# Half 0's tile table begun right behind its row numbers, its VectorE operations at low rank in the plan

## The chip, the cores and the metric

The kernel runs on one core of one Trainium2 chip. The metric is the device time of one execution in microseconds (us). The engines are named as in the profile: PE is TensorE's matmuls and PEld its weight loads, DVE is VectorE, ACT is ScalarE, POOL is GpSimd, SP is SyncE, which here only issues DMAs and reads registers. SBUF is the on-chip working memory, PSUM the small memory that PE writes its products to.

## What is computed

Attention, then a mixture of eight experts with one expert for each token, then a dense layer pair:

```python
x = attn(rotate(q), rotate(k), v)            # B, H, S, D = 2, 8, 576, 64
x = x.transpose(0, 2, 1, 3).reshape(1152, 512)
logits = x @ w_gate + modality_bias[modality_id]
e_idx = argmax(logits, axis=1)               # one of 8 experts
for e in range(8):                           # h: 512 x 1024, then 1024 x 512
    mask = e_idx == e
    out[mask] = gate_w[mask] * (relu(x[mask] @ w1[e]) @ w2[e])
h = out @ w_in                               # 512 x 2048
return (h * tanh(softplus(h))) @ w_out       # 2048 x 512
```

All in float32; products run as sums of a rounded high part and a low part ("hi" and "lo").

## The kernel before

**Stages.** Sixteen heads of attention (heads 0 to 7 are half 0 of the tokens, heads 8 to 15 half 1), then the experts for half 0 and half 1 (two tiles of 304 rows each, L712), then the dense pair (L1588, L1649).

**One head.** POOL prepares its inputs: `p_mul` (L924, 128x1152), `p_add` (L928), `p_hi` and `v_hi` (L934), `p_lo` (L943), `v_lo` (L968), all from SBUF to SBUF; `p_lo` of head n is the plan's operation ("plo", n). Then PE forms the scores (`sc`, L979) in one of two PSUM tiles, DVE takes each row's maximum (`nm`, L1003), ACT the exponential (`pexp`, L1014). PE transposes it into a buffer of a ring of three in PSUM (`pt`, L1027), ACT writes the rounded part (`ph`, L1047), DVE the rest (`pl`, or the lower rows of `ph`, L1053), which gives the ring's buffer back, and PE multiplies with the values (`av`, L1068). The same ring holds the small product `xo` (L1098), which DVE reads at L1108. POOL adds to the sums of the exponentials (`rs`, L1086).

**The plan.** The order of the attention's instructions on every engine is made ahead of the run by `Plan`, a list scheduler with assumed durations, due times (`K`) and dependencies; engines run what they are given strictly in that order. Besides its operations the plan has streams: generators that yield one step at a time. A stream whose engine is in `low` gets a slot there only if its step is thought to be over, with 0.1 us to spare, before the next operation could start:

```python
if c is None or t + (st["next"][1] - P["slack"] if e in st["low"] else 0.0) <= c[0]:
    c = (t, 0, st)
```

**Routing of half 0.** When heads 0 to 7 are done, `routing(0)` finds each token's expert and its row in a sorted buffer `scratch` (up to L404, "row numbers"); POOL then scatters the rows to it by five indirect DMAs (L410), and DVE makes the tile table `tbl` (L433 to L523), eighteen small operations on one partition: which expert and which rows each tile has. SP reads the table into registers (L555, L556) and loads rows and weights (`weights()`), when the table, the scatters and the last head's loads are done.

Up to the row numbers the intermediate tiles lie in PSUM where `near` puts them; behind `side = False` (L428) `near` returns a tile of pool `rp`, so that all tiles of half 0's table (`ce`, `n1`, `qi`, `stq`, `lt`, `te`, `cs`) and its constants (`zero`, `iotat`, `iota8`, `base`) are in SBUF:

```python
def near(sh, nm):
    if not side:
        return t(sh, nm)
    ...
    v = cur["rtile"][0:sh[0], o:o + n]
```

For half 1 (`side` stays true) most of them are views of a PSUM tile. Two tensors of SBUF are read by L439 (`ce`, `n1`), L447 (`n1`, `zero`), L453 (`qi`, `n0`), L455 (`st`, `base`), L481 (`qi`, `iotat`), L492 (`iota8`, `e8`), L497 (`lt`, `st`) and L502 (`iotat`, `cs`) of half 0; the ten others read one.

Of the kernel before, what the change touches and what calls it, by code (L numbers as in the profile page):

```python
# [18 lines left out]
B, H, S, D = 2, 8, 576, 64  # L19
# [193 lines left out]
def moe_kernel(ctx: ExitStack, tc: tile.TileContext, aps, out):  # L213
# [17 lines left out]
    def heads(x):  # L231

        return x[..., 0:XC].rearrange("p j (h e) -> p j h e", h=H)
# [343 lines left out]
    def load_rows(k):  # L577
        r = regs[k]
        pool = mp if k != "x" else wpool[-1]
        xrow[k] = t = pool.tile([128, 3, RW], F32, tag="xrow", name=f"xrow{k}")  # L580
        for i, (r0, rn) in enumerate(TCH):
            ld = nc.sync.dma_start(out=t[:rn, i], in_=scratch[ds(r["c"] + r0, rn), :])
            if k != "x":
                after_scatters(ld, k[0])
# [240 lines left out]


    def attention(actx, hook):
        a_c = actx.enter_context(tc.tile_pool(name="a_const", bufs=1))
        p2 = actx.enter_context(tc.tile_pool(name="a_p2", bufs=2))
# [404 lines left out]
        op("ids", "act", 0.1, 30.0, setup_ids)  # L1234
        op("bias", "pool", 2.5, 60.0, setup_bias, deps=[("ids",)])
        hook(plan, bank, ltile)
        plan.run()

# [12 lines left out]
    def route(b):  # L1251
        yield from routing(b, lambda: cur["rbank"]())

    def tile_rows(b):
        for i in range(2):
            regs[b, i] = tile_regs(tbl[b][:, i])

    def until_pe(gen):
        for y in gen:
            if y[0] in ("pe", "mark"):  # L1260
                return
            yield y

    def hook(plan, bank, ltile):

        r0 = route(0)
        cur["rbank"] = lambda: bank("counts")

        def until_mark():
            for y in r0:  # L1270
                if y[0] == "mark":
                    return
                yield y

        def mark(name):
            return lambda t: plan.done.update({name: ("dve", t)})

        def start():
            plan.add(until_pe(r0), plan.now, end=mark("rt"), gate=cur["spare"])

        def rest():
            next(r0)
            plan.add(until_mark(), plan.now + 1.0, end=mark("rt_row"))

        def scatter():
            plan.add(cur["scatters"], plan.now, low=("pool",), end=mark("rt_sc"))

        def table():
            plan.add(r0, plan.now, end=mark("rt_end"))

        def weights():
            tile_rows(0)
            load_rows(K0)
            feed.rows.add(K0)
            plan.done["xrow"] = ("sp", plan.now + 7.8)
            plan.add(until_pe(gen0), plan.now + 3.9, low=LOW)

        K0, n0, xg = (0, 0), B * H - 1, []

        def x_gate(i):  # L1300
            x, rn = xrow[K0], TCH[i][1]
            if not xg:
                gated.add(K0)
                t = mp.tile([128, FC1, T], F32R, tag="hl", name=f"xg{K0}").bitcast(F32)
                xg.append(t.rearrange("p a t -> p (a t)")[:, 0:3 * DM].rearrange(
                    "p (i d) -> p i d", i=3
                ))
            nc.vector.tensor_scalar(
                out=xg[0][:rn, i].rearrange("p (h e) -> p h e", h=H),
                in0=heads(x)[:rn, i, :, 0:D], scalar1=x[:rn, i, XC + 1:XC + 2], scalar2=None,  # L1310
                op0=ALU.mult,
            )

        def x_bank(c):
            return ltile[3 + c // 2][:, c % 2]

        def x_tr(c, i):
            r0, rn = TCH[i]
            nc.tensor.transpose(
                out=x_bank(c)[:, r0:r0 + rn], in_=xg[0][:rn, i, c * 128:(c + 1) * 128],  # L1320
                identity=ident[:rn, :rn],
            )

        def x_hi(c):
            if K0 not in xsplit:
                xsplit[K0] = tuple(
                    mp.tile([128, KC, T], F32R, tag=t, name=f"{t}{K0}") for t in ("xh", "xl")
                )
            nc.scalar.activation(out=xsplit[K0][0][:, c], in_=x_bank(c)[:, :T], func=AF.Copy)

        def x_lo(c):
            xh, xl = xsplit[K0]
            nc.vector.tensor_tensor(
                out=xl[:, c], in0=x_bank(c)[:, :T], in1=xh[:, c].bitcast(F32), op=ALU.subtract
            )

        def x_op(name, eng, dur, fn, *a, deps):
            plan.op((name,) + a, eng, dur, 900.0, lambda: fn(*a), deps=deps)

        for i in range(3):  # L1340
            plan.op(
                ("gate", i), "dve", 0.5, (162.0, 165.0, 150.0)[i], lambda i=i: x_gate(i),
                deps=["xrow"],
            )
        for c in range(KC):
            for i in range(3):
                x_op("xtr", "pe", 0.11, x_tr, c, i,
                     deps=[("gate", i), ("exp", n0, 1, c // 2, 3 + c // 2)])
            x_op("xhi", "act", 0.31, x_hi, c, deps=[("xtr", c, i) for i in range(3)])
            x_op("xlo", "dve", 0.39, x_lo, c, deps=[("xhi", c)])  # L1350

        z = 10.0 * H
        plan.op(
            "route", "sp", 0.0, z, start,
            deps=[("norm", n, f) for n in range(H) for f in range(2)],
        )
        plan.op("rt_mm", "pe", 0.43, z, lambda: next(r0), deps=["rt"], take=[("ring", "rt")])
        plan.op("rt_cp", "dve", 1.1, z, rest, deps=["rt_mm"], give=[("ring", "rt")])
        plan.op("scatter", "sp", 0.0, z, scatter, deps=["rt_row"])
        plan.op("table", "sp", 0.0, z, table, deps=["rt_row", ("plo", B * H - 1)])  # L1360
        plan.op(
            "rows", "sp", 2.2, z, weights,
            deps=["rt_end", "rt_sc", ("stack", B * H - 1), ("vload", B * H - 1)],
        )
# [14 lines left out]
    with ExitStack() as actx:  # L1379
        attention(actx, hook)  # L1380
# [414 lines left out]
```

## Time and profile before

| what | value |
|---|---|
| median of 3 runs | 485.11 us (484.85 to 485.18) |
| the profiled execution's own time | 485.32 us |
| its span, first to last instruction | 483.6 us |
| PE, DVE, ACT, POOL busy, us of the span | 464.2, 390.4, 331.2, 361.9 |
| half 0's row numbers ready (L397 on DVE) | 110.72 us |
| half 0's table, first and last operation | 134.29 and 145.52 us |
| last product of the attention on PE begins | 162.71 us |
| first matmul of the experts (L712) begins | 163.17 us |

Times of rows are counted from the start of the span. A row of the timeline gives start, duration, engine, line, operation, output<-input and count of merged instructions; what stands in brackets is idle time of the engine ahead of it and what ended it. Rows of one engine can overlap, since it starts the next instruction before the last one's writes have landed.

### The profile page before, as it was taken

To read this page: it belongs to the slowest core of one execution; us is meant where nothing else is said; L and a number is where in the kernel's file an instruction comes from. 1 tells how busy PE (TensorE), PEld (TensorE's weight loads), DVE (VectorE), ACT (ScalarE), POOL (GpSimd) and SP (SyncE) were. 2 spreads that over 40 slices of the span, in tenths; PEclk is the share of its full clock that TensorE was granted. 3 is DMA by queue.
4 is the path that set the end of the run, shared out by engine and by line. 5 is a ranking of instruction groups with operands and counts; after the bars stand their busy time and mean duration, and the time that the engine had idled before them with its cause. 6 is when DMAs were issued, how large, how long until landed. Compare 5 with 4: busy or idle time off the path is not lost.

```text
span 483.6 us, 8783 instructions
## 1 busy us (share of the span) xinstructions
PE 464.2 (96%) x2996; PEld 427.7 (88%) x2996; DVE 390.4 (81%) x616; ACT 331.2 (68%) x753; POOL 361.9 (75%) x363
## 2 busy tenths in 40 slices
PE   2799999999999999999999999999999999999995
PEld 1699999999998999999999998989889887888894
DVE  6599899798898765655888689999999859777773
ACT  3588888777878665475554587666675788776763
POOL 3799999999981588768767277786786749987654
PEclk9999999999999999999999999999999999999999
DMA  7689985877765399977974400202000001100002
GB/s 225 168 200 243 224 239 149 193 205 178 182 162 171 136 386 385 330 300 262 378 279 186 174 2 1 79 10 87 1 0 1 1 1 43 45 22 1 1 0 89
DMA packets 24131, 69.41 MB, mean 144 GB/s; under 512 B 5522, under 2 KB 9810, under 8 KB 22034
## 3 DMA queue, kind: packets, MB, share of 16 engines
q1 hardware_dynamic: 21794, 63.16, 42.1%
q0 software_dynamic: 1456, 5.03, 2.7%
q10 hardware_dynamic: 832, 0.61, 0.5%
q8 instruction: 25, 0.41, 0.3%
q14 instruction: 24, 0.20, 0.1%
HBM read 49.08 MB, written 6.44 MB: 115 GB/s over the span
## 4 chain that ended last, share of the span: by engine, by line
PE 41%; DVE 8%; issue 3%; POOL 1%; ACT 1%; POOLq 0%; DVEq 0%; ACTq 0%
PE h L1588 15%; PE o L1649 15%; PE mm L712 11%; DVE ta L1614 6%; DVE wc L1418 1%; DVE ta L1615 1%; POOL out_dram L1659 0%; DVE wc L1408 0%; PE mm L675 0%; DVE wc L1413 0%; POOLq L1791 0%; POOL g L1632 0%; DVE idi L1735 0%; ACT ot L1655 0%; DVE yl L1526 0%
## 5 line engine op out<-in xcount | busy, mean ns | idle before, releaser
L1614 DVE RECIPROCAL ta<-ta 128x320 f32<-128x320 f32 (+1 forms) x64 | 124.6, 1947 | 21.5 <-ACT ta L1607 20.0
L1562 POOL TENSOR_TENSOR w2l<-wc,w2h 128x512 fp32r<-128x512 f32 x64 | 89.3, 1417 | 15.3 <-ACT w2h L1561 15.3
L1649 PE MATMUL o<-w2h,g 128*128 128x512 f32 x288 | 97.8, 395 | 0.1
L1632 POOL TENSOR_TENSOR g<-ta,g 128x320 fp32r<-128x320 f32 (+1 forms) x63 | 52.7, 841 | 27.9 <-ACT g L1626 21.3
L979 PE MATMUL sc<-sk,sq 128*128 128x288 f32 (+1 forms) x320 | 59.4, 315 | 11.5 <-ACT sk L908 7.7
L1588 PE MATMUL h<-yl,w2h 128*128 128x320 f32 (+2 forms) x204 | 67.0, 328 | 0.1
L1588 PE MATMUL h<-yh,w2h 128*128 128x320 f32 (+2 forms) x204 | 66.9, 328 | 0.0
L1588 PE MATMUL h<-yh,w2l 128*128 128x320 f32 (+2 forms) x204 | 66.9, 328 | 0.0
L1649 PEld LDWEIGHTS o<-w2h,g 128*128 128x128 f32 x288 | 53.9, 188 | 12.2 <-POOL g L1632 1.0
L1047 ACT ACTIVATE ph<-pt 128x512 fp32r<-128x512 f32 (+2 forms) x112 | 54.8, 509 | 13.4 <-PE pt L1027 12.4
L1014 ACT ACTIVATE pexp<-sc,nm 128x576 f32<-128x576 f32 x72 | 53.3, 740 | 15.5 <-DVE nm L1003 11.7
L1003 DVE TENSOR_REDUCE nm<-sc 128x1 f32<-128x576 f32 x72 | 53.7, 753 | 10.8 <-PE sc L979 6.7
L979 PEld LDWEIGHTS sc<-sk,sq 128*128 128x128 f32 (+1 forms) x320 | 46.6, 190 | 14.3 <-ACT sk L908 8.1
L1649 PE MATMUL o<-w2l,g 128*128 128x512 f32 x144 | 56.8, 394 | 0.0
L1027 PE MATMUL pt<-ident,pexp 128*128 128x128 f32 (+1 forms) x360 | 55.0, 277 | 0.7 <-DVE tbl L523 0.6
L1068 PE MATMUL av<-ph,vhl 128*128 128x256 f32 (+1 forms) x160 | 50.7, 333 | 0.0
L1053 DVE TENSOR_TENSOR pl<-pt,ph 128x512 fp32r<-128x512 f32 (+1 forms) x80 | 48.8, 628 | 2.1 <-ACT ph L1047 1.8
L1027 PEld LDWEIGHTS pt<-ident,pexp 128*128 128x128 f32 (+1 forms) x360 | 42.1, 138 | 3.6 <-issue 0.7
L1626 ACT ACTIVATE g<-ta 128x320 fp32r<-128x320 f32 (+1 forms) x64 | 27.9, 436 | 22.9 <-DVE ta L1615 22.5
L1603 ACT ACTIVATE ta<-h 128x320 f32<-128x320 f32 (+1 forms) x64 | 25.5, 399 | 25.0 <-PE h L1588 23.5
L1588 PEld LDWEIGHTS h<-yl,w2h 128*128 128x128 f32 x204 | 38.3, 188 | 4.1 <-DVE yl L1526 0.4
L1588 PEld LDWEIGHTS h<-yh,w2h 128*128 128x128 f32 x204 | 38.3, 188 | 3.9 <-DVE ta L1615 0.2
(448 smaller groups left out, 1203.7 us busy)
## 6 DMA issues: line engine op xcount, KB each, us to landing
wr<-in_wio_dram SPq DMA_DIRECT2D x16, 1024.0 KB, 6.1
wc<-in_w_dram SPq DMA_DIRECT2D x26, 512.0 KB, 5.7
xs<-in_qk_dram SPq DMA_DIRECT2D x15, 576.0 KB, 5.2
sk<-ab SPq DMA_DIRECT2D x30, 288.0 KB, 3.3
sq<-ab SPq DMA_DIRECT2D x30, 144.0 KB, 2.4
vraw<-in_v_dram SPq DMA_DIRECT2D x16, 160.0 KB, 3.9
scratch<-zero SPq DMA_DIRECT2D x12, 108.8 KB, 4.8
xrow(0, 0)_2295<-scratch SPq DMA_DIRECT2D x2, 290.0 KB, 3.1
```

The costliest lines, as they stand in the source:

```text
L712: nc.tensor.matmul(ps[:, :T], lhsT=w, rhs=m, start=(n == 0), stop=(n == 3 * len(pairs) - 1))
L979: nc.tensor.matmul(t[:m, hf, :NC2], lhsT=sq[:, c:c + m], rhs=sk[:, z, hf * NC2:(hf + 1) * NC2], start=(z == 0), stop=(z == 1),)
L1003: nc.vector.tensor_reduce(out=nm[n, j], in_=sc[n, j][:, :, :NC2], axis=AX.XY, op=ALU.max, negate=True)
L1014: nc.scalar.activation(out=pe, in_=sc.pop((n, j))[:, :, :NC2], func=AF.Exp, bias=nm.pop((n, j)), accum_out=st[n, hf][:, i:i + 1],)
L1027: nc.tensor.transpose(out=t[:kn, o:o + 128], in_=pexp[n, j][:, k0:k0 + kn], identity=ident)
L1047: nc.scalar.activation(out=block(ph, n, hf, kts, slice(0, kn)), in_=psum(n, hf, kts, kn), func=AF.Copy)
L1068: nc.tensor.matmul(av[n, hf][:, :u.nq], lhsT=vhl[n][:, kt].rearrange("p a d -> p (a d)"), rhs=src[:, kt, u.at:u.at + u.nq], start=(kt == 0 ...
L1562: nc.gpsimd.tensor_tensor(out=lo[:, cs], in0=w[:, cs], in1=hi[:, cs].bitcast(F32), op=ALU.subtract)
L1588: nc.tensor.matmul(ps[:, :w], lhsT=wt[:, c], rhs=m[y][:, c], start=(n == 0), stop=(n == 11))
L1614: nc.vector.reciprocal(out=ta, in_=ta)
L1632: eng.tensor_tensor(out=gt[q][1][:, o:o + w], in0=tas.pop((q, i))[:, :w], in1=gt[q][0][:, o:o + w].bitcast(F32), op=ALU.subtract,)
L1649: nc.tensor.matmul(acc[g, t], lhsT=a[:, s], rhs=b, start=(f == 0 and z == 0), stop=(f == FC2 - 1 and z == 2),)
```

## The change

The table's stream no longer waits for ("plo", 15), the POOL preparation of the last head, but only for the row numbers, and its steps have low rank on DVE.

```diff
@@ hook()
         def table():
-            plan.add(r0, plan.now, end=mark("rt_end"))
+            plan.add(r0, plan.now, low=("dve",), end=mark("rt_end"))
...
-        plan.op("table", "sp", 0.0, z, table, deps=["rt_row", ("plo", B * H - 1)])
+        plan.op("table", "sp", 0.0, z, table, deps=["rt_row"])
```

No instruction is added or removed; the order changes on DVE, PE, ACT and POOL from there to the end of attention, and on SP it stays.

DVE behind the row numbers, in the stage of heads 10 and 11 (113 to 117 us of the profile before); names end in a buffer number. Before:

```order
L1003 TENSOR_REDUCE nm_1_1742<-sc_111 128x1
L1108 TENSOR_TENSOR X_81<-xo_1_1744,rs_1_1641 128x2x72
L1053 TENSOR_TENSOR pl_0_1748<-pt_0_0_1736,ph_0_1747 128x384
L1092 RECIPROCAL rs_0_1754<-rs_0_1754 128x3
L1003 TENSOR_REDUCE nm_3_1767<-sc_110 128x1
L1053 TENSOR_TENSOR pl_0_1748<-pt_0_1_1750,ph_0_1747 128x384
L1092 RECIPROCAL rs_0_1777<-rs_0_1777 128x3
L1053 TENSOR_TENSOR pl_0_1748<-pt_0_2_1769,ph_0_1747 128x384
```

The same place now:

```order
L433 TENSOR_REDUCE ce_1731<-cnt_1667 1x8
L437 TENSOR_SCALAR n_1736<-ce_1731 1x8
L1003 TENSOR_REDUCE nm_1_1746<-sc_111 128x1
L439 SCALAR_TENSOR_TENSOR n_1736<-ce_1731,n_1736 1x8
L1108 TENSOR_TENSOR X_81<-xo_1_1748,rs_1_1641 128x2x72
L1053 TENSOR_TENSOR pl_0_1752<-pt_0_0_1739,ph_0_1751 128x384
L1092 RECIPROCAL rs_0_1760<-rs_0_1760 128x3
L1003 TENSOR_REDUCE nm_3_1773<-sc_110 128x1
L1053 TENSOR_TENSOR pl_0_1752<-pt_0_1_1754,ph_0_1751 128x384
L1092 RECIPROCAL rs_0_1783<-rs_0_1783 128x3
L447 SCALAR_TENSOR_TENSOR qi_1759<-n_1736,zero 1x8
L1053 TENSOR_TENSOR pl_0_1752<-pt_0_2_1775,ph_0_1751 128x384
```

L433 and L437 now stand ahead of a maximum, L439 behind it and ahead of the first L1053, and L447 ahead of the third; nothing else moved there.

DVE a little later (117 to 121 us). Before:

```order
L1003 TENSOR_REDUCE nm_4_1808<-sc_111 128x1
L1053 TENSOR_TENSOR ph_0_1747<-pt_0_4_1793,ph_0_1747 64x384
L1053 TENSOR_TENSOR pl_0_1748<-pt_0_0_1803,ph_0_1747 128x2x256
L1053 TENSOR_TENSOR pl_0_1748<-pt_0_2_1810,ph_0_1747 128x2x256
L1003 TENSOR_REDUCE nm_3_1849<-sc_110 128x1
```

Now:

```order
L1003 TENSOR_REDUCE nm_4_1816<-sc_111 128x1
L453 TENSOR_TENSOR stq_1797<-qi_1759,n_1736 1x8
L455 SCALAR_TENSOR_TENSOR stq_1797<-stq_1797,base_1668 1x8
L1053 TENSOR_TENSOR ph_0_1751<-pt_0_4_1802,ph_0_1751 64x384
L1053 TENSOR_TENSOR pl_0_1752<-pt_0_0_1811,ph_0_1751 128x2x256
L1053 TENSOR_TENSOR pl_0_1752<-pt_0_2_1818,ph_0_1751 128x2x256
L1003 TENSOR_REDUCE nm_3_1860<-sc_110 128x1
```

L453 and L455 now stand between the maximum and the three L1053; the twelve later operations of the table follow in the same way up to the stage of head 14.

DVE where the table used to end (143 to 146 us). Before:

```order
L1003 TENSOR_REDUCE nm_1_2233<-sc_110 128x1
L511 TENSOR_SCALAR te_2157<-te_2157 1x10
L1003 TENSOR_REDUCE nm_0_2241<-sc_111 128x1
L516 TENSOR_SCALAR te_2157<-te_2157 1x10
L1053 TENSOR_TENSOR pl_1_2220<-pt_1_0_2207,ph_1_2219 128x512
L523 CAST tbl_2249<-te_2157 1x4
L1053 TENSOR_TENSOR pl_1_2220<-pt_1_2_2235,ph_1_2219 128x512
```

Now:

```order
L1003 TENSOR_REDUCE nm_0_2228<-sc_111 128x1
L1003 TENSOR_REDUCE nm_1_2235<-sc_110 128x1
L1053 TENSOR_TENSOR pl_1_2218<-pt_1_0_2204,ph_1_2217 128x512
L1108 TENSOR_TENSOR X_81<-xo_0_2237,rs_0_2087 128x3x72
L1053 TENSOR_TENSOR pl_1_2218<-pt_1_2_2230,ph_1_2217 128x512
```

The table's steps are gone from here.

## Rows read from the trace of the kernel before

**Rows 1.** The page's part 1: busy us (share of the span) xinstructions.

```profile
PE 464.2 (96%) x2996; PEld 427.7 (88%) x2996; DVE 390.4 (81%) x616; ACT 331.2 (68%) x753; POOL 361.9 (75%) x363
```

**Rows 2.** Stretches: length, busy PE, PEld, DVE, ACT, POOL (instructions), clock, DMA share, GB/s.

```profile
112.00:134.00 22.00, 21.87 (x174) 20.76 (x173) 19.36 (x41) 18.61 (x47) 20.76 (x22) 1.00 0.71 177
134.00:146.00 12.00, 11.43 (x93) 10.77 (x91) 11.81 (x38) 8.72 (x23) 9.06 (x18) 1.00 0.68 188
146.00:163.20 17.20, 16.73 (x134) 15.58 (x132) 14.67 (x34) 14.30 (x35) 4.41 (x6) 1.00 0.40 124
```

**Rows 3.** Waits of PE, 113 to 170 us: total us, times, longest.

```profile
PE pt L1027 <- DVE tbl L523: 0.6, 1, 0.6
```

**Rows 4.** Source view of table operations: duration ns min/median/max, start; first half 0's.

```profile
L439 DVE SCALAR_TENSOR_TENSOR n<-ce,n x1: 330/330/330, 135.6 to 135.6; 1x8 f32<-1x8 f32 x1
L439 DVE SCALAR_TENSOR_TENSOR rt<-rt,n x1: 161/161/161, 173.5 to 173.5; 1x8 f32<-1x8 f32 x1
...
L481 DVE TENSOR_TENSOR lt<-qi,iotat x1: 309/309/309, 138.9 to 138.9; 1x80 f32<-1x80 f32 x1
...
L492 DVE TENSOR_TENSOR lt<-iota,e x1: 221/221/221, 141.3 to 141.3; 1x80 f32<-1x80 f32 x1
```

**Rows 5.** Timeline of DVE at L439, and of POOL beside L439 and L481.

```profile
135.64 0.33 DVE L439 SCALAR_TENSOR_TENSOR n<-ce,n 1x8 f32<-1x8 f32 x1
...
135.09 0.86 POOL L968 TENSOR_TENSOR vhl<-vraw,vhl 128x320 fp32r<-128x320 f32 x1
...
138.69 0.46 POOL L934 TENSOR_SCALAR vhl<-vraw 128x320 fp32r<-128x320 f32 x1
```

**Rows 6.** Source view of L1413 and L1562, and both in the timeline at 300 us.

```profile
L1413 DVE SCALAR_TENSOR_TENSOR wc<-wr,wc x4: 1348/2261/2305, 300.8 to 366.0; 128x1024 int32<-128x1024 int32 x4
...
L1562 POOL TENSOR_TENSOR w2l<-wc,w2h x64: 1277/1298/2294, 274.2 to 463.5; 128x512 fp32r<-128x512 f32 x64
...
300.79 2.30 DVE L1413 SCALAR_TENSOR_TENSOR wc<-wr,wc 128x1024 int32<-128x1024 int32 x1
...
300.70 3.53 POOL L1562 TENSOR_TENSOR w2l<-wc,w2h 128x512 fp32r<-128x512 f32 x2
```

**Rows 7.** Timeline of DVE, 113 to 119 us.

```profile
113.53 0.76 DVE L1003 TENSOR_REDUCE nm<-sc 128x1 f32<-128x576 f32 x1 [0.27 <-PE sc L979]
114.20 0.30 DVE L1108 TENSOR_TENSOR X<-xo,rs 128x144 f32<-128x144 f32 x1
114.42 0.55 DVE L1053 TENSOR_TENSOR pl<-pt,ph 128x384 fp32r<-128x384 f32 x1
...
116.27 0.99 DVE L1053 TENSOR_TENSOR pl<-pt,ph 128x384 fp32r<-128x384 f32 x2
117.18 0.75 DVE L1003 TENSOR_REDUCE nm<-sc 128x1 f32<-128x576 f32 x1
118.23 0.55 DVE L1053 TENSOR_TENSOR ph<-pt,ph 64x384 fp32r<-64x384 f32 x1 [0.30 <-ACT ph L1047]
```

**Rows 8.** Timeline of POOL, 113 to 122 us.

```profile
113.89 1.42 POOL L928 TENSOR_TENSOR xs<-xs 128x576 f32<-128x576 f32 x1
...
116.75 1.42 POOL L943 TENSOR_TENSOR ab<-xs,ab 128x576 fp32r<-128x576 f32 x1
...
118.96 2.67 POOL L924 TENSOR_TENSOR xs<-xs,tabs 128x1152 f32<-128x1152 f32 x1
121.56 0.49 POOL L934 TENSOR_SCALAR vhl<-vraw 128x320 fp32r<-128x320 f32 x1
```

**Rows 9.** Timeline of PE, the transposes that wait for the ring.

```profile
115.11 0.85 PE L1027 MATMUL pt<-ident,pexp 128*128 128x128 f32 x6
...
117.25 1.04 PE L1027 MATMUL pt<-ident,pexp 128*128 128x128 f32 x8
...
119.24 0.38 PE L1027 MATMUL pt<-ident,pexp 128*64 128x128 f32 x2
```

**Rows 10.** Source view of L1408, a DVE operation with one input.

```profile
L1408 DVE TENSOR_SCALAR wc<-wr x4: 769/1294/1778, 294.9 to 360.1; 128x1024 int32<-128x1024 int32 x4
```

## The prediction

> **What bounds the kernel now.** I read the page first: PE is busy for 96% of the span [rows 1], so time is gained or lost only where PE stands still. Then the stretches around the change: from 112 to 163 us, the second half of attention, PE lacks 0.13, 0.57 and 0.47 us of the three stretches [rows 2]. That is the first thing to see: all that a better order could win there is about 1.2 us, and any wait that is put into PE's stream costs its full length, since behind it PE has no idle time to give back. The waits of PE name one place that the table has to do with: 0.6 us on a transpose, put down to L523, the table's last step [rows 3]. The second thing is how DVE and POOL share these stretches. From 112 to 134 us DVE is busy for 19.36 of 22 us and POOL for 20.76; from 134 to 146 DVE is full (11.81 of 12) and POOL only at three quarters [rows 2]. The table runs before in the second of these; the change moves most of it into the first.
>
> **What is removed.** The eighteen steps leave the full stretch, and the third order piece shows the L1053 that gives the ring's buffer back no longer behind L511 and L516. I take the wait of 0.6 us for gone: -0.6, its bounds being -0.6 and 0.
>
> **What is moved.** No instruction is new, so the question is what the steps cost at their new places. Alone they are cheap: 0.15 to 0.25 us from start to end [rows 4], less in DVE's stream, since the next instruction begins before the end. That DVE has 2.6 us idle in the new stretch [rows 2] would cover them. But two of half 0's rows are longer than they should be. L439 takes 330 ns, and the same step of half 1, with PSUM for one of its tensors, 161; L481 takes 309, and L492, of the same shape, 221 [rows 4]. Both stretched ones stand beside a POOL instruction that reads SBUF and both end about when it does: L439 begins at 135.6 and is over at 135.97, POOL's L968 runs from 135.09 to 135.95; L481 runs from 138.9 to 139.2, POOL's L934 from 138.69 to 139.15 [rows 4, 5]. They lost only 0.2 and 0.1 us because they met the last bit of a short instruction. Larger operations show the whole of it: L1413 with both inputs in SBUF takes 1.35 us at best and 2.30 when POOL's L1562 began 0.09 us ahead of it; two L1562, 1.28 us each at best, then take 3.53 together [rows 6]. The sum fits only if DVE stood until the first POOL instruction was over (1.28 - 0.09 = 1.19, plus some 1.15 of work) and the second POOL instruction then stood until DVE was done. So a DVE instruction with two SBUF inputs and a POOL instruction that reads SBUF run one after the other, and whoever comes second waits. Eight of the table's steps have two SBUF inputs (L439, L447, L453, L455, L481, L492, L497, L502). In their old place the other six fell into POOL's scatters or its pauses; in the new one POOL works on SBUF almost without pause.
>
> Now the walk through the first two order pieces, with POOL at its old times, since its preparation there waits for nothing that DVE makes.
>
> *L439.* It gets the slot in which L1108 began, 114.20 [rows 7]. POOL's L928 runs from 113.89 to 115.31 [rows 8]. DVE goes on at 115.31: 1.11 late. The L1053 of 114.42 then ends at 116.08 instead of 114.97 [rows 7]. It gives back the ring's buffer that the transposes of 115.11 need, and these began 0.14 after its end [rows 9], so there is no slack: PE +1.11.
>
> *L447.* Its slot is 116.27 + 1.11 = 117.38 [rows 7]. POOL's L943 runs until 118.17 [rows 8]: 0.79 more, DVE is 1.90 late. The L1053 behind it (the first of two in 0.99 us) ended near 116.82 and its buffer goes to the transposes of 117.25 [rows 7, 9]; with the 0.14 from above the slack is 0.29. PE +1.61.
>
> *L453 and L455.* The maximum of 117.18 passes DVE on after 0.67, as that of 113.53 does [rows 7]; the slot is 117.85 + 1.90 = 119.75. POOL's L924, its longest instruction, runs from 118.96 to 121.63 [rows 8]. L455 needs what L453 writes, and by then L934 has POOL's turn, until 122.05 [rows 8]. The next L1053 began at 118.23 and begins at 122.05: 3.82 late. It ended at 118.78, its buffer goes to the transposes of 119.24 [rows 7, 9], slack 0.32. PE +3.50.
>
> *L481, L492, L497, L502.* Each costs nothing where POOL pauses, and up to 1.42 (L928 and L943) where it has just begun [rows 8]: 0 to 5.7 together. POOL is less dense by then. In the new order an addition of L1086, which needs an exponential of the delayed heads, stands ahead of POOL's L943 and holds it, and DVE has idle time of its own left from the 2.6 us. I take +0.3, near the low end.
>
> *The ten steps with one input* I cost at nothing: none of the rows above shows them in a wait, and DVE's idle time covers some 0.1 us each; without it they would be 1 us.
>
> *What is queued behind.* DVE's in-order stream is the price itself. On SP the table's register reads come earlier, but the loads behind them still wait for the scatters, and nothing else of the attention stands behind them: 0. POOL's later preparation and its scatters come late by about as much as PE does, so the experts' rows keep their distance to the end of attention: 0. PE's and ACT's order is changed in small pieces from head 13 on (two scores back to back, four products put ahead of a score); each can open or close a gap of some tenths, 0 +- 0.5.
>
> **Sum.** +3.5 + 0.3 - 0.6 = +3.2 us against the profiled execution's 485.32, or 488.5; that execution lies 0.2 above the median of 485.11, so 488.3.
>
> **The rivals.** A change of 0.2%, 0.97 us, is about what a measurement of this kernel can tell from none: 484.14 to 486.08 is the same.
>
> *The steps don't wait for POOL, not slower.* L439 and L481 are operations on one partition, and their stretch is 0.17 and 0.09 us; it could be another delay, and the long waits at 300 us are of 128 partitions. Then the steps fall into DVE's idle time and only the 0.6 us at L523 goes: 484.5. Against it: both ends meet POOL's ends, and none of the other six, whose neighbours on POOL read no SBUF tensor, is stretched. It decides as soon as L439 passes in under 0.2 us at 114.2 while L928 runs.
>
> *Fewer waits.* The dearest term hangs on L453 meeting L924. If POOL is some 0.8 us later than before, or DVE earlier, L453 slips in ahead of it, and only L439 and L447 are paid: 1.61 + 0.3 - 0.6 = +1.3, 486.4.
>
> *More waits.* Steps with one input can wait too. L1408 reads one SBUF tensor and takes 0.77 us at best and 1.78 at worst [rows 10]. Six steps of the table are of that kind or a cast (L437, L490, L507, L511, L516, L523; L461 handles one element). If every second one meets a POOL instruction of 1.42 [rows 8], at its middle, that is 6 x 0.5 x 0.7 = 2.1 more: 490.4. The Trainium skill, page "SBUF — State Buffer", section "Who interferes with whom", says just this: a copy, cast or tensor_scalar in a two-port mode takes the pair of ports that DVE shares with GpSimd, and the second to issue is blocked until the first is done. By that rule the sum would be 490.4; the row of L1408 agrees with it for a large operation, and no row shows it for one of ten elements.
>
> **How the numbers follow.** The waits as walked, 486.9 to 489.8: 0.58, likeliest 488.3. Fewer, 485.9 to 486.9: 0.14. More, 489.8 to 492: 0.13. None, 484.0 to 485.3: 0.15. The range 485.5 to 491.0 takes in the first two and the nearer half of the third and leaves out about 0.2; the first case's own is 486.9 to 489.8. Faster by over 0.2% needs the "none" case and a gap or two more closed: 0.04. Within 0.2%: the rest of it and the low edge of "fewer", 0.14. Slower: 0.82.
>
> **What would show it.** In the profile after, L439 should begin near 114.2 and end with POOL's L928, over 1 us long; L447 and L453 should likewise end with L943 and L924. PE should have waits on DVE at the transposes (L1027) between 115 and 123 us, 3 to 4 us in all, and L712 should begin near 166.4 instead of 163.17. The wait at L523 should be gone. From L712 on all should stand as before, only later. I am wrong if L439 is 0.15 us long beside L928, if PE's waits in this stretch stay under 1 us, or if the time is lost behind L712.

## The result, and the profile after

The changed kernel takes 490.74 us, the median of 5 runs (489.53 to 491.42), against 485.11 (484.85 to 485.32): ratio 1.011, 95% interval 1.0099 to 1.0121. It is slower by 5.6 us, on the forecast's side and inside its range, and further than its likeliest value. The profiled execution took 490.42 us with a span of 488.7, 5.1 above that of before.

The page's part 1, which answers to [rows 1]:

```profile
PE 466.1 (95%) x2996; PEld 429.6 (88%) x2996; DVE 395.3 (81%) x616; ACT 332.4 (68%) x753; POOL 361.0 (74%) x363
```

DVE has the same 616 instructions and is busy for 4.9 us more: a step that is held counts as busy, so what it waits for has to be found beside it. The source view of the table's steps in the changed kernel (duration in ns min/median/max, start); each appears once for half 0:

```profile
L439 DVE SCALAR_TENSOR_TENSOR n<-ce,n x1: 1122/1122/1122, 114.2 to 114.2; 1x8 f32<-1x8 f32 x1
L447 DVE TENSOR_TENSOR_SCAN qi<-n,zero x1: 990/990/990, 117.2 to 117.2; 1x8 f32<-1x8 f32 x1
L453 DVE TENSOR_TENSOR stq<-qi,n x1: 1902/1902/1902, 119.7 to 119.7; 1x8 f32<-1x8 f32 x1
L455 DVE SCALAR_TENSOR_TENSOR stq<-stq,base x1: 160/160/160, 121.7 to 121.7; 1x8 f32<-1x8 f32 x1
...
L497 DVE TENSOR_TENSOR lt<-lt,stq x1: 1492/1492/1492, 135.3 to 135.3; 1x80 f32<-1x80 f32 x1
...
L502 DVE SCALAR_TENSOR_TENSOR cs<-iotat,cs x1: 384/384/384, 137.1 to 137.1; 1x10 f32<-1x10 f32 x1
...
L511 DVE TENSOR_SCALAR te<-te x1: 722/722/722, 138.2 to 138.2; 1x10 f32<-1x10 f32 x1
```

What POOL did beside them, from its timeline in the same execution (start, duration):

```profile
113.88 1.42 POOL L928 TENSOR_TENSOR xs<-xs 128x576 f32<-128x576 f32 x1
...
116.75 1.42 POOL L943 TENSOR_TENSOR ab<-xs,ab 128x576 fp32r<-128x576 f32 x1
...
118.95 2.66 POOL L924 TENSOR_TENSOR xs<-xs,tabs 128x1152 f32<-128x1152 f32 x1
123.10 0.46 POOL L934 TENSOR_SCALAR vhl<-vraw 128x320 fp32r<-128x320 f32 x1 [1.50 <-PE av L1068]
...
135.23 1.44 POOL L928 TENSOR_TENSOR xs<-xs 128x576 f32<-128x576 f32 x1
...
137.51 1.41 POOL L943 TENSOR_TENSOR ab<-xs,ab 128x576 fp32r<-128x576 f32 x1
```

Add start and duration in both lists. L439 is over at 115.32 and L928 at 115.30; L447 at 118.20, L943 at 118.17; L453 at 121.62, L924 at 121.61; L497 at 136.76, L928 at 136.67; L511 at 138.95, L943 at 138.92. Steps of eight to eighty elements on one partition end 0.01 to 0.09 us after a POOL instruction, however long that one still had to run. POOL keeps the times of before [rows 8] up to L924.

What PE paid, from its timeline, the four transposes that found the ring's buffer not given back (in brackets the idle time ahead and what ended it):

```profile
116.15 0.84 PE L1027 MATMUL pt<-ident,pexp 128*128 128x128 f32 x6 [1.14 <-DVE rs L1092]
...
118.72 1.12 PE L1027 MATMUL pt<-ident,pexp 128*128 128x128 f32 x8 [0.28 <-DVE pl L1053]
...
122.45 0.41 PE L1027 MATMUL pt<-ident,pexp 128*64 128x128 f32 x2 [1.49 <-DVE ph L1053]
...
139.46 0.98 PE L1027 MATMUL pt<-ident,pexp 128*128 128x128 f32 x6 [1.44 <-DVE pl L1053]
```

The first three answer to [rows 9], where the same transposes start at 115.11, 117.25 and 119.24: PE comes to them 1.04, 1.47 and 3.21 us later. (The releaser L1092 of the first is the instruction beside the L1053 that PE needed.) A fifth wait, 0.16 us, is at 123.17, where PE is 3.56 us later (119.61 before). That is more than the waits in brackets add up to, 3.07, since before, the transposes at 117.25, 119.24 and 119.61 start some 0.15 us ahead of the end of the matmul before them, and behind a wait they do not.

One more loss does not show as a wait. The windows view of the changed kernel, behind the third wait: length, busy PE, PEld, DVE, ACT, POOL, granted clock, DMA share, GB/s.

```profile
118.70:122.50 3.80, 2.29 (x17) 1.99 (x18) 3.70 (x6) 2.34 (x7) 2.90 (x2) 1.00 0.85 176
...
123.20:127.70 4.50, 4.50 (x23) 4.21 (x24) 3.83 (x8) 2.35 (x6) 2.66 (x4) 0.62 0.55 174
127.70:138.00 10.30, 10.30 (x83) 9.92 (x81) 9.47 (x22) 7.65 (x20) 8.35 (x9) 1.00 0.42 93
```

PE is busy for all of the 4.5 us, but its mean granted clock is 0.62: it had stood still for 1.5 of the 3.8 us before, and then ran for some 3.4 us, from 123.6, at the lower of its two levels (1.2 and 2.4 GHz). By the clock that is 4.5 x 0.38 = 1.7 us of work lost. A score of four matmuls takes 1.31 us there instead of 0.78. The same stretch of matmuls in both profiles, first the changed kernel's:

```profile
123.86 1.52 PE L1098 MATMUL xo<-mov,avt 128*128 128x72 f32 x6
125.13 1.31 PE L979 MATMUL sc<-sk,sq 128*128 128x288 f32 x4
...
128.59 0.70 PE L979 MATMUL sc<-sk,sq 128*128 128x288 f32 x4
...
140.20 0.78 PE L979 MATMUL sc<-sk,sq 128*128 128x288 f32 x4
```

And the kernel before:

```profile
120.31 0.87 PE L1098 MATMUL xo<-mov,avt 128*128 128x72 f32 x6
...
123.57 0.69 PE L979 MATMUL sc<-sk,sq 128*128 128x288 f32 x4
```

PE is 3.55 us later at the L1098 and 5.02 later at the second L979, so it lost 1.47 us between them without a wait: that is the measured price of the clock here.

At the end of the attention the first matmul of the experts begins at 168.67 us, 5.50 later than before. The parts: the delay by the waits up to 123 us 3.56; the clock 1.47; the wait at 139 us 1.44; less the wait behind L523, 0.57, which is gone, and 0.22 at the last product of the attention (0.25 instead of 0.47). Together 5.7, or 0.2 too much; what makes up for it in PE's changed order stays open. Some 0.4 us come back in the dense pair: before, two neighbouring matmuls of L1649 start at 356.52 and 357.07, and in the changed kernel the same two follow within 0.23 us.

### The profile page after: what moved, and what is told of

Same layout as the page of the kernel before. It is cut to its first block, busy times and chain, and to the rows that moved or that the text cites. A ratio compares the mean times of both kernels' runs of the same rounds, so it can differ in the third digit from the quotient of the medians.

```text
span 488.7 us, 8779 instructions
## 1 busy us (share of the span) xinstructions
PE 466.1 (95%) x2996; PEld 429.6 (88%) x2996; DVE 395.3 (81%) x616; ACT 332.4 (68%) x753; POOL 361.0 (74%) x363
## 4 chain that ended last, share of the span: by engine, by line
PE 52%; POOL 0%; issue 0%; ACT 0%; POOLq 0%; DVE 0%
PE h L1588 20%; PE o L1649 20%; PE mm L712 11%; POOL out_dram L1659 0%; PE mm L675 0%; POOLq L1791 0%; ACT ot L1655 0%; DVE yl L1526 0%; ACT yh L1524 0%; ACT Y L762 0%; POOL spacer L1666 0%; POOLq L1659 0%
## 5 line engine op out<-in xcount | busy, mean ns | idle before, releaser
L1562 POOL TENSOR_TENSOR w2l<-wc,w2h 128x512 fp32r<-128x512 f32 x64 | 90.3, 1432 | 16.5 <-ACT w2h L1561 16.5
L1649 PE MATMUL o<-w2h,g 128*128 128x512 f32 x288 | 97.7, 395 | 0.0
L1632 POOL TENSOR_TENSOR g<-ta,g 128x320 fp32r<-128x320 f32 (+1 forms) x63 | 51.7, 825 | 27.7 <-ACT g L1626 21.0
L979 PE MATMUL sc<-sk,sq 128*128 128x288 f32 (+1 forms) x320 | 59.8, 316 | 11.6 <-ACT sk L908 7.8
L1649 PEld LDWEIGHTS o<-w2h,g 128*128 128x128 f32 x288 | 54.0, 188 | 11.6 <-POOL g L1632 0.2
L1003 DVE TENSOR_REDUCE nm<-sc 128x1 f32<-128x576 f32 x72 | 53.6, 752 | 10.2 <-PE sc L979 6.1
L979 PEld LDWEIGHTS sc<-sk,sq 128*128 128x128 f32 (+1 forms) x320 | 47.0, 192 | 13.9 <-ACT sk L908 8.1
L1649 PE MATMUL o<-w2l,g 128*128 128x512 f32 x144 | 56.8, 394 | 0.0
L1053 DVE TENSOR_TENSOR pl<-pt,ph 128x512 fp32r<-128x512 f32 (+1 forms) x80 | 48.9, 628 | 2.5 <-ACT ph L1047 2.1
L1588 PEld LDWEIGHTS h<-yh,w2l 128*128 128x128 f32 x204 | 38.4, 188 | 2.3
```

Source lines behind the costliest of these rows:

```text
L979: nc.tensor.matmul(t[:m, hf, :NC2], lhsT=sq[:, c:c + m], rhs=sk[:, z, hf * NC2:(hf + 1) * NC2], start=(z == 0), stop=(z == 1),)
L1003: nc.vector.tensor_reduce(out=nm[n, j], in_=sc[n, j][:, :, :NC2], axis=AX.XY, op=ALU.max, negate=True)
L1562: nc.gpsimd.tensor_tensor(out=lo[:, cs], in0=w[:, cs], in1=hi[:, cs].bitcast(F32), op=ALU.subtract)
L1588: nc.tensor.matmul(ps[:, :w], lhsT=wt[:, c], rhs=m[y][:, c], start=(n == 0), stop=(n == 11))
L1632: eng.tensor_tensor(out=gt[q][1][:, o:o + w], in0=tas.pop((q, i))[:, :w], in1=gt[q][0][:, o:o + w].bitcast(F32), op=ALU.subtract,)
L1649: nc.tensor.matmul(acc[g, t], lhsT=a[:, s], rhs=b, start=(f == 0 and z == 0), stop=(f == FC2 - 1 and z == 2),)
```

## The experiments

**The theory:** a DVE step that needs SBUF in a certain way and a POOL instruction that reads SBUF take turns, and the time goes where DVE came second. **The rivals:** any extra step in front of the instructions that give the ring back costs this; the early table costs in itself (its register reads, the loads behind it); and, as part of the theory, one-input steps wait too.

### Stand-ins at the new places

The kernel before with its table where it was, and eighteen steps of unused results where the changed kernel's table runs (the plan sees the same durations and rank). Three kinds: as the table's (stand_as_is), all as reductions (stand_reduce), and only the two-input ones as reductions (stand_one).

```diff
+        def stand_in():
...
+            for k, x in zip("RSTTTTSTRSTTRTSSSC", (a, a, a, a, a, a, a, b, c, c, b, b, c, c, c, c, c, c)):
+                yield "dve", 0.12, True
+                z = zero[0:1, 0:x.shape[1]]
+                if k == "T" and True:      # False in stand_reduce, stand_one
+                    V.tensor_tensor(out=x, in0=z, in1=zero[0:1, 80:80 + x.shape[1]], op=ALU.add)
+                elif k in "SC" and True:   # False in stand_reduce
+                    V.tensor_scalar(out=x, in0=z, scalar1=0.0, scalar2=None, op0=ALU.add)
+                else:
+                    V.tensor_reduce(out=x, in_=z[:, :, None], axis=AX.X, op=ALU.add)
...
+        plan.op("stand_in", "sp", 0.0, z, lambda: plan.add(stand_in(), plan.now, low=("dve",)), deps=["rt_row"])
```

> The kernel before, its table at its old place, and eighteen stand-in steps of the same kinds and sizes (reading and writing SBUF only, their results unused) put where the changed kernel's table runs. If the price of the change is turn-taking between DVE steps and POOL's SBUF instructions, it is paid here too: the first two-input stand-ins last 1 to 2 us each beside L928, L943 and L924, PE waits about 3 us between 115 and 123 us, and the time is 489 to 491.5 us. If the price came from the earlier table itself (its register reads, the rows loaded earlier), it stays within 0.5 us of before: 484.7 to 485.7.

> The same eighteen stand-ins in the same places of the plan, but each a TENSOR_REDUCE with one SBUF input. Turn-taking by operands: a reduction was never stretched in the traces (0.20 to 0.22 us), so no step is over 0.3 us, PE has no wait of 1 us, and the time is 484.8 to 486.0 us. If instead any eighteen extra steps ahead of the instructions that give the ring back cost this much, because DVE is full there, the time is 489 or more, as for the stand-ins as they are.

> The same, with the seven one-input TENSOR_SCALAR and cast steps kept as TENSOR_SCALAR with SBUF input and output, and the eight two-input ones as reductions. If TENSOR_SCALAR waits for POOL too, as the 0.72 us of L511 beside L943 suggests, the stand-ins that meet a POOL instruction last 0.3 to 1.4 us and the time is 0.5 to 2 us above that of the reductions. If only two-input steps wait, all steps last under 0.2 us and the time is that of the reductions, within 0.3 us.

Measured: stand_as_is 490.74 us, ratio 1.0114 (1.0097 to 1.0131), the same as the changed kernel. stand_reduce 485.63, ratio 1.0008 (0.9998 to 1.0017), no difference that can be told. stand_one 486.47, ratio 1.0023 (1.0015 to 1.0032). The source view of the stand-ins, stand_as_is:

```profile
L1298 DVE TENSOR_TENSOR d<-zero x8: 153/776/1906, 114.8 to 137.4; 1x8 f32<-1x8 f32 x4, 1x80 f32<-1x80 f32 x3, 1x10 f32<-1x10 f32 x1
...
L1300 DVE TENSOR_SCALAR d<-zero x7: 140/165/722, 113.9 to 156.8; 1x10 f32<-1x10 f32 x5, 1x8 f32<-1x8 f32 x2
```

stand_reduce, all eighteen:

```profile
L1302 DVE TENSOR_REDUCE d<-zero x18: 120/142/214, 113.1 to 149.5; 1x10 f32<-1x10 f32 x8, 1x8 f32<-1x8 f32 x7, 1x80 f32<-1x80 f32 x3
```

stand_one, the seven with one input and the eleven reductions:

```profile
L1300 DVE TENSOR_SCALAR d<-zero x7: 140/176/1206, 113.7 to 151.1; 1x10 f32<-1x10 f32 x5, 1x8 f32<-1x8 f32 x2
...
L1302 DVE TENSOR_REDUCE d<-zero x11: 120/141/216, 113.6 to 131.1; 1x8 f32<-1x8 f32 x5, 1x80 f32<-1x80 f32 x3, 1x10 f32<-1x10 f32 x3
```

The rival of the order falls: eighteen extra steps in the same slots are free if they are reductions. So does that of the early table, to within about 1 us: the price is paid with the real table at its old place, where PE's wait of 0.6 us behind L523 stays as well. What costs is the kind of step. And TENSOR_SCALAR with one SBUF input belongs to the costly kinds (up to 1.21 us), about 0.8 us of time for its seven steps here.

### Probes in an order that does not move

The kernel before with one extra DVE step of unused result behind each of 31 row maxima (L1003) of heads 3 to 9; four kinds of step, shown as the line of each.

```diff
+            if 3 <= n < 10:
+                nc.vector.tensor_tensor(out=probe, in0=iotat[0:1, 0:8], in1=zero[0:1, 0:8], op=ALU.add)
# probe_psum:   nc.vector.tensor_tensor(out=probe, in0=sc[n, j][0:1, 0, 0:8], in1=zero[0:1, 0:8], op=ALU.add)
# probe_one:    nc.vector.tensor_scalar(out=probe, in0=zero[0:1, 0:8], scalar1=0.0, scalar2=None, op0=ALU.add)
# probe_single: nc.vector.tensor_scalar(out=probe[:, 0:1], in0=zero[0:1, 0:1], scalar1=0.0, scalar2=None, op0=ALU.add)
```

> The kernel before with one extra DVE step of 1x8 behind each of the 31 row maxima (L1003) of heads 3 to 9, an addition of two SBUF constants whose result is unused; nothing else in the order moves. Turn-taking: POOL works on SBUF for most of these heads (instructions of 0.5 to 2.7 us), so the probe waits for what is left of one in perhaps two of three places: median 0.3 to 1.0 us, longest over 2 us, together 15 to 30 us of DVE, 10 to 25 us of it on PE: 495 to 510 us. If the stretched steps in the changed kernel had another cause than POOL, the probes take 0.15 to 0.2 us each, and the time is under 487.

> The same probe with one of its two inputs in PSUM (the score tile whose maximum was just taken), the other in SBUF. Turn-taking by two SBUF inputs: none waits, all under 0.25 us, 31 x 0.1 us of DVE, mostly hidden: 485 to 487 us. If the number of inputs counts and not where they are, it is as slow as the probe with both in SBUF.

> The same probe as a TENSOR_SCALAR of 1x8 with one SBUF input and SBUF output. After L490 of the kernel that is only early (2.36 us beside L924) and L511 of the changed one (0.72 us beside L943) it should wait as the two-input one does: 490 to 510 us, longest over 2 us. If those two were stretched for another reason, its steps take 0.15 us and the time is 485 to 487.

> The one-input probe with one element instead of eight. L461, of one element, lasted 0.14 us beside L928 and 0.13 beside L943 where longer TENSOR_SCALAR steps waited. If one element is served without POOL's turn, all 31 probes take under 0.2 us and the time is 485 to 486.5; if L461 was lucky, it is near 499 like the probe with eight.

Measured, with the source view of the probe (ns min/median/max). probe_two, both inputs in SBUF, 499.57 us, ratio 1.0293 (1.0271 to 1.0315):

```profile
L1009 DVE TENSOR_TENSOR probe<-iotat,zero x31: 143/362/2369, 39.3 to 113.0; 1x8 f32<-1x8 f32 x31
```

probe_psum, one of them in PSUM, 485.71 us, ratio 1.0007 (0.9996 to 1.0017):

```profile
L1009 DVE TENSOR_TENSOR probe<-sc,zero x31: 143/144/147, 39.7 to 98.4; 1x8 f32<-1x8 f32 x31
```

probe_one, one input, 499.22 us, ratio 1.0286 (1.0262 to 1.031):

```profile
L1009 DVE TENSOR_SCALAR probe<-zero x31: 149/382/2373, 39.4 to 111.4; 1x8 f32<-1x8 f32 x31
```

probe_single, one input of one element, 485.16 us, ratio 1.0003 (0.9994 to 1.0013):

```profile
L1009 DVE TENSOR_SCALAR probe<-zero x31: 130/131/133, 39.5 to 98.4; 1x1 f32<-1x1 f32 x31
```

This measures the disputed cost by itself. The same eight-element addition takes 143 to 147 ns every time with one operand in PSUM and up to 2.37 us with both in SBUF; 31 of these make the kernel 14 us slower. The one-input TENSOR_SCALAR is as dear, and free with a single element.

That it is POOL which they wait for shows in the timelines. Of probe_two's 31 steps, 22 begin 0.04 us or more behind the start of a POOL instruction that has more than 0.14 us to go, and every one of them is over 0 to 0.02 us after that instruction; the nine others take 0.14 to 0.18 us, six of them in POOL's pauses. A free step and the longest one, with POOL's row:

```profile
68.81 0.14 DVE L1009 TENSOR_TENSOR probe<-iotat,zero 1x8 f32<-1x8 f32 x1
...
70.43 2.37 DVE L1009 TENSOR_TENSOR probe<-iotat,zero 1x8 f32<-1x8 f32 x1
```

```profile
70.14 2.64 POOL L924 TENSOR_TENSOR xs<-xs,tabs 128x1152 f32<-128x1152 f32 x1
```

In probe_psum a step in the middle of the same POOL instruction is not held:

```profile
58.78 0.14 DVE L1009 TENSOR_TENSOR probe<-sc,zero 1x8 f32<-1x8 f32 x1
```

```profile
57.33 2.67 POOL L924 TENSOR_TENSOR xs<-xs,tabs 128x1152 f32<-128x1152 f32 x1
```

### One part of the change alone

early_only: the start moved up, the rank as before. low_only: low rank, the start as before.

```diff
# early_only, against the changed kernel
-            plan.add(r0, plan.now, low=("dve",), end=mark("rt_end"))
+            plan.add(r0, plan.now, end=mark("rt_end"))
# low_only, against the changed kernel
-        plan.op("table", "sp", 0.0, z, table, deps=["rt_row"])
+        plan.op("table", "sp", 0.0, z, table, deps=["rt_row", ("plo", B * H - 1)])
```

> The changed kernel with the table's start moved up but its steps at their old rank: all eighteen stand between 113 and about 128 us, one between every two of the attention's instructions. Turn-taking: POOL is busy with SBUF instructions for nearly all of it, so more steps wait than with low rank: 490 to 494 us. If low rank is what does the harm (steps put off into worse places), this is faster than the changed kernel: under 488.

> Only the low rank, the start at its old place behind the last head's preparation. In the order the table now ends only seven DVE instructions ahead of the experts' row scaling (L1308), since the full stretch from 134 to 146 us leaves it few slots; the loads that need it come late, and PE waits for them at the end of the attention: L712 3 to 8 us later, 487 to 493 us, with no step over 0.5 us and no wait on DVE in the ring. If low rank were free where POOL is at rest, it is 484 to 485.5.

early_only: 489.29 us, ratio 1.0071 (1.0045 to 1.0097); neither side's number (490 or more, under 488). The table is over at 127.9 us, and most steps slipped through. Two rows of DVE and two of POOL, from the timelines, show the luck:

```profile
116.00 0.14 DVE L453 TENSOR_TENSOR stq<-qi,n 1x8 f32<-1x8 f32 x1
...
119.28 2.36 DVE L490 TENSOR_SCALAR e<-te 1x10 f32<-1x10 f32 x1
```

```profile
115.98 0.70 POOL L934 TENSOR_SCALAR ab<-xs 128x576 fp32r<-128x576 f32 x1
...
118.97 2.65 POOL L924 TENSOR_TENSOR xs<-xs,tabs 128x1152 f32<-128x1152 f32 x1
```

L453, the dearest step of the changed kernel, met L934 at its very start and lost nothing; L490, with one input, met L924 and lost 2.2 us. PE's mean granted clock between 124 and 134 us is 0.66 in this profile. Four executions were timed: 490.30 and 490.60 us with a mean clock of 0.990 over the run, 487.87 and 488.29 with 0.999. So the same order differs by some 2.4 us, and the mean clock goes with it; that the two faster ones kept the full clock behind the waits is not shown, since only the first was profiled.

low_only: 495.19 us, ratio 1.0204 (1.0182 to 1.0227), the slowest version of the table, and with no step stretched (L497 takes 0.20 us). PE's waits from 110 to 180 us:

```profile
PE sc L1319 <- DVE xg(0, 0)_2508 L1308: 3.9, 1, 3.9
PE mm L712 <- DVE xl(0, 0)_2525 L1333: 2.6, 1, 2.6
```

In the full stretch the plan has few slots for a stream of low rank; L523 comes at 157.9 us instead of 145.5, the experts' rows are loaded too late, and PE waits at the end of the attention. The mechanism is as expected, the time 2 us past the range: the expectation had no term for the clock, and PE's is at 0.50 to 0.63 from 164 to 176 us, where L712 takes 0.46 us a matmul instead of 0.30. In the changed kernel, with its early start, there is no such wait.

### Steps only in POOL's pauses, and the changed kernel again

Two attempts at a version that beats both: the early start with the old rank, but until the last preparation is done a step may start only when the plan has POOL idle (pauses), or idle within 0.1 us (pauses2).

```diff
-            plan.add(r0, plan.now, low=("dve",), end=mark("rt_end"))
+            plan.add(r0, plan.now, end=mark("rt_end"),
+                     gate=lambda t: ("plo", 15) in plan.done or plan.free["pool"] <= t)
# pauses2:                                              ... or plan.free["pool"] <= t + 0.1)
```

> The same with no 0.1 us of allowance: only the first step comes a little early, the table runs three or four instructions ahead of its old places: 484.3 to 485.5, with or without the wait of 0.6 us behind the last step.

> The table may begin behind the row numbers, its steps at their old rank, but as long as the last head's preparation is not done a step gets a slot only when the plan has POOL idle, or idle within 0.1 us. So three steps come early and the others from about 130 us on, a few places ahead of where they were before. If turn-taking is the price, steps in POOL's pauses cost little: no step over 0.7 us, 484.3 to 486.5. If being early costs in itself, 487 or more. Since the plan's POOL times are assumed ones, a step can still miss its pause and pay up to 2.5 us.

> The changed kernel again, for its spread: runs in which the granted clock stays at 1.0 should lie 1 to 2 us under those in which it falls behind PE's waits (3.4 us at 1.2 GHz lose 1.7 us of work). 489 to 492 us. If the clock has no part in it, time and mean clock show no relation.

pauses: 488.2 us, ratio 1.0068 (1.0055 to 1.008); pauses2: 487.71, ratio 1.0047 (1.0034 to 1.006). Both expectations of a time near or under that of before were wrong. In pauses L437 still lasts 1.15 us, having missed its pause. And the split of the experts' first weights on POOL (L613) begins at 156.24 instead of 158.55, and now meets the scaling of the experts' rows (L1309 here, L1308 before; three steps, the first at 154.05). The later two steps in the timeline of DVE, POOL's row, and the same row of the kernel before:

```profile
156.62 2.27 DVE L1309 TENSOR_SCALAR xg(0, 0)_2409<-xrow(0, 0)_2277 128x512 f32<-128x512 f32 x1
158.90 0.45 DVE L1309 TENSOR_SCALAR xg(0, 0)_2409<-xrow(0, 0)_2277 128x512 f32<-128x512 f32 x1
```

```profile
156.24 2.36 POOL L613 TENSOR_TENSOR wlo(0, 0)_0_2421<-wraw(0, 0)_0_2336,whi(0, 0)_0_2355 128x1024 fp32r<-128x1024 f32 x1 [2.67 <-ACT whi(0, 0)_0_2355 L608]
```

```profile
158.55 2.37 POOL L613 TENSOR_TENSOR wlo(0, 0)_0_2467<-wraw(0, 0)_0_2358,whi(0, 0)_0_2371 128x1024 fp32r<-128x1024 f32 x1 [2.09 <-ACT whi(0, 0)_0_2371 L608]
```

The second scaling waits 1.8 us for L613 and PE 0.85 for it: the same turn-taking, at a step that nobody moved on purpose. It explains only a part. In pauses L712 begins 2.8 us later than before, and PE's waits from 110 us on are 0.9 us longer in all; in pauses2, where no step of the table is over 0.66 us, it is as late. The rest stays open, and pauses2's time is on the side of its expectation that reads "being early costs in itself". For these two orders that is not ruled out. No version that ran beats the kernel before.

after_again: 490.5 us, ratio 1.0104 (1.0089 to 1.0118), so the result repeats. The part of this expectation on the clock is not borne out cleanly: of nine executions of the changed kernel the fastest two, 489.37 and 489.53, have mean clocks of 0.997 and 1.000, but 491.42 has 0.996 and 490.42 0.993. That the lower clock costs about 1.5 us in the profiled execution rests on its rows. The profiles of after_again and stand_as_is show the same drop to 0.50, from about 124 to 127 us, behind the same waits; before, stand_reduce and stand_one, without a wait over 0.2 us from 110 to 128 us, stay at 1.00 there.

## Why the prediction was right, and where its sizes were off

**The waits as walked** were right, step by step. L439 was to begin near 114.2 and end with L928, L447 and L453 to end with L943 and L924; they do, within 0.1 us. PE was to be 1.11, 1.61 and 3.50 us late behind the three; it was 1.04, 1.47 and 3.21 late. The last is smaller mainly because L455 did not have to wait for L934: POOL itself stood for 1.50 us, waiting for PE, so that L934 came at 123.10 and not at 121.56, and the L1053 behind L455 was 3.61 us late instead of 3.82:

```profile
121.84 0.55 DVE L1053 TENSOR_TENSOR ph<-pt,ph 64x384 fp32r<-64x384 f32 x1
```

That POOL's preparation "waits for nothing that DVE makes" failed there, in the kernel's favour: the PE product that it waited for was late by DVE.

**That the mechanism is turn-taking by operands** was argued from two small stretches and one pair of long instructions [rows 4 to 6]; the probes and stand-ins show it.

**The wait behind L523** is gone, as forecast: -0.57.

**Two terms were too small.** First, "L481, L492, L497, L502: +0.3" and "the ten steps with one input: nothing". L497 met L928 just at its start (1.49 us), L502 and L511 lost a little more, and PE waited 1.44 at 139 us. From the rows DVE came late there by 1.3, 0.2 and 0.55 us, and about 0.6 of that was covered, so the two-input step was most of it. L511, with one input, is what my rival "more waits" was about. The Trainium skill, page "SBUF — State Buffer", section "Who interferes with whom", counts tensor_scalar among the operations that can enter a two-port mode and then block or be blocked, and says that tensor_reduce never contends on this chip. The runs agree on both counts: probe_one up to 2.37 us, and stand_reduce's eighteen steps all at 0.12 to 0.21 us. I had held against the rule that no row showed it for ten elements. Eight were held for the whole rest of the POOL instruction; a single one was not held.

Second, the clock. The sum counted what PE waits and not what it loses afterwards: 1.47 us at 1.2 GHz behind the third wait. Without this term the profiled execution would lie at 489.0, near the 488.5 of the sum; that they are so close is in part chance, since the sum had 0.3 us for what became the 1.44 at 139 us, and nothing for the 0.4 us that come back in the dense pair.

**So the time, 490.74, came out where the third rival had put it (489.8 to 492)**, by its mechanism only in small part: the two-input steps gave 3.56 and most of 1.44, the clock 1.47. It is above the first case's own 486.9 to 489.8, and no case had a term for the clock; that the stated range holds it owes as much to the range's width as to the sum. The rivals "no waits" and "fewer waits" fell with L439 and L453.

**Behind L712**, which begins at 168.67 and not near 166.4, all stands as before, later by 5.5 us at first and 5.1 at the end. That the register reads and loads on SP cost PE nothing holds: behind the start of L712 the list of PE's waits has the same single entry in both profiles, 0.3 us put down to L1500.

**Not tried:** keeping the operands of half 0's table in PSUM, as half 1 does for most of them. probe_psum shows the effect only on a step that reads a tile just used by DVE.

## What to carry to other kernels

Before a small DVE step is moved "into idle time", look at what POOL runs at that moment and where the step's operands lie: with two SBUF inputs, or as a TENSOR_SCALAR from SBUF to SBUF, a step of eight elements lasted here until POOL's SBUF instruction was over. One operand in PSUM, or a reduction in its place, made it free. A wait of PE is then to be priced with the clock behind it, and a plan that knows only durations will keep offering such slots.

## What the runs showed of the hardware that was not expected

A TENSOR_SCALAR of one element was never stretched: 31 of 31 took 130 to 133 ns, some in the middle of POOL's L924, beside which eight elements took up to 2373. L461, the only such step of the table, took 130 to 141 ns in each profiled order of the table.

Which of the two came first is decided within some hundredths of a microsecond, as far as these rows show. In early_only L453 begins 0.02 us after the row of POOL's L934, is not held, and L934 lasts 0.70 instead of 0.67 us. A step of probe_two at 84.15 us that begins 0.02 us after a POOL row passes likewise, in 0.18 us; L497 of the changed kernel, 0.04 us after the row of L928, is held to its end.

Behind waits of 1.1, 0.3, 1.5 and 0.2 us within 9 us, PE's granted clock was at 1.2 GHz from 123.6 us for 3.4 us, with PE busy all the while; behind one wait of 1.4 us at 139 us, with PE busy for 15 us before, it stayed at 2.4 GHz.
